# Padding of K and Q by DMA instead of Pool memsets, and a first LayerNorm in four batches, in a fused attention and GeGLU block

## Chip, cores and metric

One core of a Trainium2 chip. The metric is the device time of one execution in microseconds (us). Every kernel was run several times beside the kernel before on the same chip. Ratios are computed as the mean time of one kernel's fast runs over the mean of the other's fast runs of the same rounds, so they are not quite the ratios of the medians that are quoted. The kernel before differed from one section of runs to the next by up to 0.3% (medians 945.7 to 948.9 us, both on the same chip). This goes with the mean granted clock of PE that each run lists: over all sections 14 of its runs at 1.000 took 945.6 to 946.9 us, 10 at 0.998 took 947.1 to 948.0 and 10 at 0.996 took 948.9 to 949.2. So the ratios, and the times of events within a trace, carry the argument, not small differences of medians from different sections; and a ratio that is off 1 by a few tenths of a per cent says something only where both kernels ran at the same clock.

## The reference, cut to what matters

```python
# x: [1, 2048, 640] bf16; H = 32 heads of Dh = 20; Df = 1728
def reference(x, wqkv, wo, w_gate, w_up, w_down):
    n = layernorm(x)                                  # "LN1" below
    q, k, v = split_heads(n @ wqkv)                   # 32 heads x 2048 x 20
    p = softmax(q @ k.T * 20 ** -0.5)
    h = x + merge_heads(p @ v) @ wo
    m = layernorm(h)
    return h + (gelu(m @ w_gate) * (m @ w_up)) @ w_down
```

## The kernel before

The program is written as a list of operations with priorities. A list scheduler orders them for each engine with estimated durations before the program is built. The order on each engine is then fixed, and every engine works strictly in that order (in e5 below, LN1's third tile was ready at 14.57 us, but its transposes ran at 18.87, behind V projections that waited for their weights until 17.03).

K and Q lie transposed in SBUF. Partitions are used in four blocks of 32, one head in each: row 32j holds a bound, rows 32j+1 to 32j+20 the head's 20 values, rows 32j+21 to 32j+31 are padding. The padding must be written before the first scores are computed (0 in Q and about 1 in K). Heads come in 8 groups (`NG`); group 0 is started first.

```python
kt_all = sb("kt_all", [128, NG, S])            # K: 8 groups x 4 KB a partition
qt_all = sb("qt_all", [128, 4, NG, 512])       # Q: 4 chunks x 8 groups x 1 KB a partition

def fills(g0, g1, c0, c1):                     # Pool memsets of whole tiles, padding included
    v = lambda ap: ap.bitcast(FP32)
    n = g1 - g0
    cst(I("memset", v(kt_all[:, g0:g1, :].rearrange("p g s -> p (g s)")), ones2), "ktm%d" % g0, 1024 * n)
    for c in range(c0, c1):
        cst(I("memset", v(qt_all[:, c, g0:g1, :].rearrange("p g s -> p (g s)")), 0.0), "qtm%d%d" % (c, g0), 256 * n)

fills(0, 1, 0, 1)                              # group 0 first
# ... small constants ...
fills(1, NG, 0, 1)                             # then the rest of K and of Q's chunk 0
for c in range(1, 4):                          # and Q's chunks 1 to 3
    cst(I("memset", qt_all[:, c, :, :].rearrange("p g s -> p (g s)").bitcast(FP32), 0.0), "qtm%d" % c, 256 * NG)
# ...
def load(dst, src, key, mb, after=(), writes=None):          # all loads on the SP queue
    return op("sp", I("dma_start", dst, src), 0.08, P_BG, writes=writes or [key], after=after,
              sem=key, lat=2.2 + mb / 0.25)                  # the scheduler's estimate of the landing
for i in range(4):
    load_x(i)                                                # 0.65 MB each
load(wqk, A_wqkv[:, 0:1280]..., "wqk", 1.6)
load(wv, A_wqkv[:, 1280:1920]..., "wv", 0.8)
load(wo[:], ..., "wo", 0.8)
# ... LN1: statistics, scale and shift ("apply"), transposes through PE
for t0, n, eng in ((0, 4, "act"), (4, 4, "act"), (8, 8, "dve")):
    for t in range(t0, t0 + n):
        ln_stats(x_sb[:, t, :], t, [f"x{t // 4}"], P_BG)     # on DVE
    ln_rsqrt(t0, n, P_EPI, True)                             # square root on ScalarE
    for t in range(t0, t0 + n):
        e_ops.append(ln_apply(eng, x_sb[:, t, :], xn_p[:, t % 4, :], ("xnp", t % 4), t, [f"x{t // 4}"], P_EPI))
        transposes(xn_p[:, t % 4, :], [("xnp", t % 4)], xnT[:, :, t * 128:(t + 1) * 128], ("xnT", t),
                   ALLB, P_EPI, "act")                       # 5 PE transposes, then one evacuation
# ... projections of K and Q for group 0, rows moved into place by DMA
dma(kt_all[32 * j + 1:32 * j + 21, 0, 512 * c:512 * c + 512], src[DH * j:DH * j + DH, :], ...)   # per j and c
dma(qt_all[32 * j + 1:32 * j + 21, 0, 0, :], q_un[DH * j:DH * j + DH, 0, :], ("q", 0, 0, j), [("qu", 0), "qtm00"], ...)
# ... the bound add, the last step before the first scores: row 32j of group 0
op("dve", lambda eng: eng.scalar_tensor_tensor(out=qt_all[:, 0, 0, :], in0=bank(bk), scalar=off0[:, 0:1], in1=dst, ...),
   ..., reads=[key, "off0"] + q_keys[0][0], ...)
```

After this prologue ScalarE computes 719 exponentials of up to 1536 columns, one after the other, and a feed-forward tail follows.

## Time and profile before

| | kernel before |
|---|---|
| time, median of 4 runs | 946.96 us (946.62 to 947.25) |
| span of the profiled run | 943.9 us |
| ScalarE busy | 881.4 us (93%) |
| first exponential | 41.46 us after the span's start |
| last K evacuation of LN1 on ScalarE | 35.47 us |
| V weights landed | about 17.3 us |

The page of the kernel before, parts 1 and 4: busy time of each engine, and the chain of work that ended last, by engine.

```profile
PE 852.4 (90%) x10332; PEld 367.6 (39%) x10388; DVE 829.6 (88%) x1804; ACT 881.4 (93%) x789; POOL 17.9 (2%) x26
...
ACT 70%; PE 17%; DVE 12%; issue 0%; DMA 0%; DVEq 0%
```

Three engines look busy, but the chain is ScalarE's: whatever delays its first exponential delays the end by the same amount, as long as it runs without gaps afterwards. The timeline of ScalarE before, end of the prologue (columns: start, duration, engine, line, operation, output and input, count; in brackets the idle time before it and what ended it):

```profile
35.47 0.60 ACT L619 ACTIVATE regw<-ps 128x512 bf16<-128x512 f32 x1 [0.41 <-PE ps L592]
36.09 1.28 ACT L339 ACT_TABLE_LOAD   x1
41.46 4.62 ACT L339 ACTIVATE pts<-ps 128x1536 bf16<-128x1536 f32 x4 [4.09 <-PE ps L829]
```

The first line is the last K evacuation of LN1, the third the first exponentials. The whole prologue is the time to 41.46 us. The timeline of DVE and Pool before, in LN1:

```profile
6.00 6.08 POOL L339 MEMSET kt_all<- 128x7168 f32 x1
...
9.37 2.73 DVE L339 CAST mv<-mv 128x8 bf16<-128x8 f32 x1
...
12.13 7.18 POOL L339 MEMSET qt_all<- 128x1792 f32 x4
12.14 1.61 DVE L339 TENSOR_SCALAR sd<-mv 128x4 bf16<-128x4 bf16 x1
```

A cast of 8 elements takes 2.73 us: it stands still until Pool's memset of K ends at 12.08 us, and the next one waits for the first memset of Q. These stalls are what the change wants to remove. The timeline of PE before:

```profile
15.72 1.53 PE L556 MATMUL ps<-ident,rege 128*128 128x128 bf16 x10 [15.72 <-ACT rege L339]
17.32 2.02 PE L592 MATMUL ps<-regw 128*128 128x320 bf16 x7
```

After the transposes of the first two tiles, PE's fixed order has V projections (320 columns), and those start when the V weights have landed, at 17.3 us. The windows view before (columns as its first line says; the last is what the DMA engines moved):

```profile
core 0: us, PE busy (x) PEld busy (x) DVE busy (x) ACT busy (x) POOL busy (x), PEclk, DMA share, GB/s
8.00:19.00 11.00, 3.11 (x17) 1.90 (x18) 10.68 (x30) 4.46 (x7) 10.77 (x5) 1.00 1.01 357
19.00:33.00 14.00, 13.04 (x117) 8.49 (x118) 12.39 (x47) 12.47 (x22) 0.31 (x1) 1.00 0.04 9
112.00:118.00 6.00, 5.28 (x65) 1.36 (x57) 6.00 (x16) 6.00 (x7) 0.00 (x0) 1.00 0.51 113
```

Until 19 us the loads of x and of the weights keep all 16 DMA engines busy at 357 GB/s. Then the DMA engines are free. The last line is a transfer to 20 neighbouring partitions.

### The profile page before, as it was taken

The page shows a single profiled execution, that of the slowest core. Times are in us where ns is not written, and L with a number is a line of the kernel's source. Part 1 is how long each engine was busy: PE and PEld are TensorE (multiplying, and loading weights), DVE is VectorE, ACT ScalarE, POOL GpSimd, SP SyncE. Part 2 cuts the span into 40 slices and gives each one's busy share as a digit, 9 for nine tenths or more (in the row PEclk, how much of TensorE's full clock was granted, in tenths as well). Part 3 has the DMA queues.
Part 4 walks back from the last instruction along what each step waited for, and adds up shares of the span by engine and source line. Part 5 has one row for each costly group of instructions (what it writes and reads, how often), then busy time and mean ns, then how long its engine had stood idle before and what let it go on. Part 6 is the DMA issues. An engine that isn't in the chain of part 4 may idle for free.

```text
span 943.9 us, 23617 instructions
## 1 busy us (share of the span) xinstructions
PE 852.4 (90%) x10332; PEld 367.6 (39%) x10388; DVE 829.6 (88%) x1804; ACT 881.4 (93%) x789; POOL 17.9 (2%) x26
## 2 busy tenths in 40 slices
PE   2999999998898999998898997999999899999998
PEld 1533232222232223232243333344434446566577
DVE  8849999999799997988799999798999989989953
ACT  3799999999999999999999999999999999999931
POOL 7000000000000000000000000000000000000000
PEclk9999999999999999999999999999999999999999
DMA  7121102325500000001000000001100000000000
GB/s 250 51 73 35 52 15 67 92 59 156 181 1 1 1 1 1 1 15 42 1 3 1 2 1 1 1 2 30 30 1 2 2 15 18 3 17 10 3 22 16
DMA packets 22047, 30.13 MB, mean 32 GB/s; under 512 B 1964, under 2 KB 19464, under 8 KB 21944
## 3 DMA queue, kind: packets, MB, share of 16 engines
q1 hardware_dynamic: 21944, 28.63, 9.8%
q8 instruction: 81, 1.33, 0.6%
q14 instruction: 22, 0.18, 0.1%
HBM read 20.12 MB, written 8.09 MB: 30 GB/s over the span
## 4 chain that ended last, share of the span: by engine, by line
ACT 70%; PE 17%; DVE 12%; issue 0%; DMA 0%; DVEq 0%
ACT pts L339 45%; ACT rege L339 24%; PE ps L592 4%; DVE rege L339 4%; PE ps L1006 4%; PE ps L829 3%; PE ps L339 2%; PE ps L1057 2%; DVE rege L789 2%; DVE qt_all L339 2%; ACT L339 1%; DVE regw L622 1%; DVE stats L339 1%; PE ps L556 1%; DMA rege<-in_A_x_dram 0%
## 5 line engine op out<-in xcount | busy, mean ns | idle before, releaser
L339 ACT ACTIVATE pts<-ps 128x1536 bf16<-128x1536 f32 x480 | 572.2, 1368 | 8.4 <-PE ps L829 5.1
L829 PE MATMUL ps<-qt_all,kt_all 32*128 32x256 bf16 (+2 forms) x3584 | 304.0, 289 | 47.4 <-ACT pts L339 29.2
L339 ACT ACTIVATE rege<-ps 128x1536 bf16<-128x1536 f32 x239 | 298.9, 1369 | 1.7 <-PE ps L339 1.6
L829 PEld LDWEIGHTS ps<-qt_all,kt_all 32*128 32x128 bf16 x3584 | 96.0, 92 | 274.6 <-ACT pts L339 161.4
L339 DVE TENSOR_TENSOR qt_all<-qt_all 128x1024 bf16<-128x1024 bf16 (+1 forms) x240 | 164.1, 684 | 3.2
L1006 PE MATMUL ps<-rege,regw 128*128 128x256 bf16 (+2 forms) x955 | 146.4, 287 | 12.8 <-ACT rege L339 4.8
L339 PE MATMUL ps<-pts,v_all 128*21 128x256 bf16 (+2 forms) x2098 | 138.8, 290 | 0.9 <-DVE rege L339 0.5
L789 DVE TENSOR_SCALAR rege<-ps 128x512 int16<-128x512 f32 x154 | 105.4, 684 | 30.1 <-PE ps L829 29.1
L339 DVE TENSOR_SCALAR qt_all<-qt_all 128x1024 bf16<-128x1024 int16 (+1 forms) x288 | 115.6, 418 | 2.0
L339 PE MATMUL ps<-rege,v_all 128*21 128x256 bf16 (+2 forms) x1294 | 113.3, 292 | 0.0
L1006 PEld LDWEIGHTS ps<-rege,regw 128*128 128x128 bf16 x980 | 72.8, 98 | 63.4 <-issue 21.2
L592 PE MATMUL ps<-regw 128*128 128x320 bf16 (+1 forms) x342 | 81.5, 348 | 3.5 <-ACT regw L562 0.8
L1057 PE MATMUL ps<-regw,rege 128*128 128x320 bf16 x448 | 78.0, 301 | 1.9 <-DVE rege L1046 0.8
L339 PE MATMUL ps<-kt_all,zer 128*32 128x512 bf16 x824 | 70.6, 384 | 0.1
L789 DVE TENSOR_SCALAR qt_all<-ps 128x512 int16<-128x512 f32 x96 | 65.6, 685 | 3.2 <-PE ps L829 2.2
L339 DVE TENSOR_SCALAR rege<-rege 128x1024 int16<-128x1024 int16 (+2 forms) x166 | 67.3, 422 | 1.0
L339 DVE TENSOR_TENSOR rege<-rege 128x1024 bf16<-128x1024 bf16 (+3 forms) x103 | 66.1, 644 | 1.0
L339 PEld LDWEIGHTS ps<-pts,v_all 128*21 128x21 bf16 x2098 | 50.2, 91 | 38.4 <-issue 30.3
L1057 PEld LDWEIGHTS ps<-regw,rege 128*128 128x128 bf16 x448 | 36.9, 98 | 32.6 <-issue 15.2
L339 PEld LDWEIGHTS ps<-rege,v_all 128*21 128x21 bf16 x1294 | 41.1, 91 | 19.8 <-issue 14.3
L592 PEld LDWEIGHTS ps<-regw 128*128 128x128 bf16 x360 | 29.0, 98 | 45.9 <-issue 21.2
L1046 DVE TENSOR_TENSOR rege<-rege,ps 128x512 bf16<-128x512 bf16 (+1 forms) x53 | 35.8, 677 | 10.5 <-PE ps L1006 9.7
(86 smaller groups left out, 611.4 us busy)
## 6 DMA issues: line engine op xcount, KB each, us to landing
rege<-in_A_x_dram SPq DMA_DIRECT2D x6, 640.0 KB, 5.1
q_rows<-regw SPq DMA_DIRECT2D x20, 128.0 KB, 1.7
out_dram<-rege SPq DMA_DIRECT2D x16, 160.0 KB, 2.1
regw<-in_B_w_gate_dram SPq DMA_DIRECT2D x1, 2160.0 KB, 10.4
regw<-in_B_w_up_dram SPq DMA_DIRECT2D x1, 2160.0 KB, 15.4
regw<-in_B_w_down_dram SPq DMA_DIRECT2D x1, 2080.0 KB, 20.6
kt_all<-k_rows SPq DMA_DIRECT2D x12, 160.0 KB
qt_all<-q_rows SPq DMA_DIRECT2D x12, 160.0 KB
```

The source lines that it names most:

```text
L339: return lambda eng: getattr(eng, method)(*args, **kwargs)
L556: op("pe", lambda eng, a=a: eng.transpose(bank16(bk, D)[:, 128 * a:128 * a + 128], src[:, a * 128:(a + 1) * 128], ident[:]), 0.055, prio, ...
L592: yield op("pe", lambda eng, l=l, r=r, k=k: eng.matmul(bank(bk, n), l, r, start=(k == 0), stop=(k == len(steps) - 1)), c_mm(n), prio, mode ...
L622: e = op("dve", lambda eng: eng.tensor_copy(dst, bank(bk)), c_dve(512), prio, reads=[key], writes=[dkey], rel=[bk], after=after)
L789: d_ops.append(op("dve", lambda eng: eng.tensor_scalar(v[:, 512 * h:512 * h + 512], bank(b), EXP_MUL, -32000.0, ALU.mult, ALU.max), c_dve( ...
L829: return lambda eng: eng.matmul(out()[:, kk * nq:(kk + 1) * nq], kt_all[32 * j:32 * j + 32, g, kt * 128:(kt + 1) * 128], qt_all[32 * j:32 ...
L1006: op("pe", lambda eng, a=a, f=f, fi=fi: eng.matmul(bank(bk)[:, fi * nq:(fi + 1) * nq], w[:, a, F0[f]:F0[f] + 128], hnT[:, a, 128 * tb:128 ...
L1046: hdone.append(op("dve", lambda eng, bu=bu, fv=fv, w=w: eng.tensor_tensor(fv, fv, bank(bu, w), ALU.mult), c_dve(w), p, reads=[ku, ("ha", k ...
L1057: op("pe", lambda eng, f=f, o=o, hf=hf, bk=bk: eng.matmul(bank(bk, 320), ha_f[:, o:o + 128], wd[:, f, hf * 320:(hf + 1) * 320], start=(f = ...
```

## The change

Its intent: free DVE from the memsets by letting DMA copy the padding of group 0 to the other groups, start LN1's applies earlier with smaller batches, and share LN1's work more evenly between ScalarE and DVE. The diff, cut to its core:

```diff
-P_QK, P_PV, P_EPI, P_BG = 0, 1, 2, 3
+P_QK, P_PV, P_PRO, P_EPI, P_BG = 0, 1, 1.5, 2, 3
 ...
-        fills(0, 1, 0, 1)
+        cst(I("memset", kt_all[:, 0, :].bitcast(FP32), ones2), "ktm0", 1024)
+        cst(I("memset", qt_all[:, 0, 0, :].bitcast(FP32), 0.0), "qtm0", 256)
 ...
-        fills(1, NG, 0, 1)
-        for c in range(1, 4):
-            cst(I("memset", qt_all[:, c, :, :].rearrange("p g s -> p (g s)").bitcast(FP32), 0.0), "qtm%d" % c, 256 * NG)
 ...   (after the loads of x and the weights, on the same queue)
+        pad_rows = [(0, 1)] + [(32 * j + DH + 1, min(32 * j + 33, 128)) for j in range(4)]
+        k_fill = [("kfill", i) for i in range(len(pad_rows))]
+        q_fill = [("qfill", j) for j in range(4)]
+        for key, (a, b) in zip(k_fill, pad_rows):
+            op("sp", I("dma_start", kt_all[a:b, 1:NG, :], kt_all[a:b, 0:1, :].to_broadcast([b - a, NG - 1, S])), 0.72, P_BG,
+               reads=["ktm0"], writes=[key], sem="kf", lat=6.0)
+        for j, key in enumerate(q_fill):
+            a, b = 32 * j + DH + 1, 32 * j + 32
+            op("sp", I("dma_start", qt_all[a:b].rearrange("p c g s -> p (c g) s")[:, 1:4 * NG, :],
+                       qt_all[a:b, 0, 0:1, :].to_broadcast([b - a, 4 * NG - 1, 512])), 0.72, P_BG,
+               reads=["qtm0"], writes=[key], sem="qf", lat=4.0)
 ...
-        for t0, n, eng in ((0, 4, "act"), (4, 4, "act"), (8, 8, "dve")):
-            for t in range(t0, t0 + n):
-                ln_stats(x_sb[:, t, :], t, [f"x{t // 4}"], P_BG)
-            ln_rsqrt(t0, n, P_EPI, True)
+        for t0 in (0, 4, 8, 12):
+            if t0 == 4:
+                act_stats(4, 4)          # sums of x and x*x by two ScalarE passes a tile
+            else:
+                for t in range(t0, t0 + 4):
+                    ln_stats(x_sb[:, t, :], t, [f"x{t // 4}"], P_BG)
+            ln_rsqrt(t0, 4, P_PRO, sqrt=True)
 ...                                     # applies all on DVE; tiles 13 and 15 evacuated by DVE
+                           ALLB, P_PRO, "dve" if t in (13, 15) else "act")
 ...   (bound add of group 0: its tile is the source of the Q fills)
-               reads=[key, "off0"] + q_keys[0][0], writes=[("qo", 0, 0)], rel=[bk])
+               reads=[key, "off0"] + q_fill + q_keys[0][0], writes=[("qo", 0, 0)], rel=[bk])
 ...
-            proj_v(kt, 0, (6, 7), P_BG, "dve")
+            proj_v(kt, 0, (6, 7), P_EPI if kt < 8 else P_BG, "dve")
```

Later K and Q rows wait for `k_fill` and `q_fill` where they waited for the memsets.

More of the change, by code (lines that the diff above doesn't have):

```diff
@@ L360, in bass_sequential_preLN__mha_block__glu_gated_geglu__prompt_kernel @@
         rs = sb("rs", [128, NT], FP32)
-        nm = sb("nm", [128, NT], FP32)
+        nm = sb("nm", [128, 2], FP32)
+        asum = sb("asum", [128, 2, 4], FP32)
         mu = sb("mu", [128, NT], FP32)
@@ L408, in bass_sequential_preLN__mha_block__glu_gated_geglu__prompt_kernel @@
         xn_p = carve(4 * D).rearrange("p (i d) -> p i d", i=4)
+        junk = rege[:, 16000:16000 + D]
         carve = carver(rege, E_WORDS)
@@ L453, in bass_sequential_preLN__mha_block__glu_gated_geglu__prompt_kernel @@
         ones2 = 1.0019378662109375
-        def fills(g0, g1, c0, c1):
-            v = lambda ap: ap.bitcast(FP32)
-            n = g1 - g0
-            cst(I("memset", v(kt_all[:, g0:g1, :].rearrange("p g s -> p (g s)")), ones2), "ktm%d" % g0, 1024 * n)
-            for c in range(c0, c1):
-                cst(I("memset", v(qt_all[:, c, g0:g1, :].rearrange("p g s -> p (g s)")), 0.0), "qtm%d%d" % (c, g0), 256 * n)
-        fills(0, 1, 0, 1)
+        cst(I("memset", kt_all[:, 0, :].bitcast(FP32), ones2), "ktm0", 1024)
+        cst(I("memset", qt_all[:, 0, 0, :].bitcast(FP32), 0.0), "qtm0", 256)
         cst(I("memset", sel[:], -1.0), "sel", 160)
@@ L508, in ln_stats, with ln_rsqrt @@
             return [a, b]
-        def ln_rsqrt(t0, n, prio, need_nm=False, table=False):
+        def ln_rsqrt(t0, n, prio, table=False, sqrt=False):
             y = rs[:, t0:t0 + n]
@@ L519, in ln_rsqrt @@
             d(I("tensor_copy", mu[:, t0:t0 + n], mv16[:, 0:n, 0]), ["mv16"], [("mu", t) for t in ts])
-            if need_nm:
+            if sqrt:
                 op("act", I("activation", sd16[:, 0:n], sd16[:, 0:n], ACT.Sqrt), 0.2, prio, reads=["sd16"], writes=["sd16"])
                 d(I("reciprocal", y, sd16[:, 0:n]), ["sd16"], rk)
-                d(I("scalar_tensor_tensor", out=nm[:, t0:t0 + n], in0=y, scalar=-1.0, in1=mu[:, t0:t0 + n],
-                    op0=ALU.mult, op1=ALU.mult), rk + [("mu", t) for t in ts], [("nm", t) for t in ts])
                 return
@@ L574, in bass_sequential_preLN__mha_block__glu_gated_geglu__prompt_kernel, with act_stats @@
         ALLB = (7, 6, 0, 1, 2, 3, 4, 5)
-        for t0, n, eng in ((0, 4, "act"), (4, 4, "act"), (8, 8, "dve")):
+        def act_stats(t0, n):
             for t in range(t0, t0 + n):
-                ln_stats(x_sb[:, t, :], t, [f"x{t // 4}"], P_BG)
-            ln_rsqrt(t0, n, P_EPI, True)
-            for t in range(t0, t0 + n):
-                e_ops.append(ln_apply(eng, x_sb[:, t, :], xn_p[:, t % 4, :], ("xnp", t % 4), t, [f"x{t // 4}"], P_EPI))
+                for f, k in ((ACT.Copy, 0), (ACT.Square, 1)):
+                    op("act", I("activation", junk, x_sb[:, t, :], f, accum_out=asum[:, k, t - t0:t - t0 + 1]), 0.72, P_BG,
+                       reads=[f"x{t // 4}"], writes=["junk", ("as", t)])
+            m = mv[:, t0:t0 + n, 0]
+            rk = [("as", t) for t in range(t0, t0 + n)]
+            d = lambda fn, r, w: op("dve", fn, 0.17, P_EPI, reads=r, writes=w)
+            d(I("tensor_scalar", m, asum[:, 0, 0:n], 1.0 / D, None, ALU.mult), rk, ["am"])
+            d(I("tensor_tensor", asum[:, 0, 0:n], m, m, ALU.mult), ["am"], rk)
+            d(I("scalar_tensor_tensor", out=mv[:, t0:t0 + n, 1], in0=asum[:, 1, 0:n], scalar=1.0 / D, in1=asum[:, 0, 0:n],
+                op0=ALU.mult, op1=ALU.subtract), rk + ["am"], [("mv", t) for t in range(t0, t0 + n)])
+        for t0 in (0, 4, 8, 12):
[5 more added lines that the diff above has]
+            ln_rsqrt(t0, 4, P_PRO, sqrt=True)
+            for t in range(t0, t0 + 4):
+                e_ops.append(ln_apply("dve", x_sb[:, t, :], xn_p[:, t % 4, :], ("xnp", t % 4), t, [f"x{t // 4}"], P_PRO))
                 transposes(xn_p[:, t % 4, :], [("xnp", t % 4)], xnT[:, :, t * 128:(t + 1) * 128], ("xnT", t),
-                           ALLB, P_EPI, "act")
+                           ALLB, P_PRO, "dve" if t in (13, 15) else "act")
                 e_ops.append(len(sc.ops) - 2)
@@ L635, in proj_k @@
                             f"kc{c}", 2.2, prio)
-                dma(kdr[128 * t:128 * t + 128, 512 * c:512 * c + 512], src, ("kdr", t, c), [("ku", t % 2, c)], f"kw{c}", 2.7,
+                dma(kdr[128 * t:128 * t + 128, 512 * c:512 * c + 512], src, ("kdr", t, c), [("ku", t % 2, c)], f"kw{t % 2}{c}", 2.7,
                     max(prio, P_BG) if t == 0 else prio, 0.4)
@@ L658, in proj_k @@
                         kdr.rearrange("(g j e) s -> j e g s", j=4, e=DH)[j, :, g0:g1, :], ("k", t, j),
-                        [("kdr", tt, c) for tt in (t - 1, t) for c in range(4)] + ["ktm1"], f"k{t}", 2.2 + 1.0 * (g1 - g0), prio, keep=False)
+                        [("kdr", tt, c) for tt in (t - 1, t) for c in range(4)] + k_fill, f"k{t}", 2.2 + 1.0 * (g1 - g0), prio, keep=False)
             op("dve", I("tensor_reduce", kd[:, t:t + 1], ka[:, 0:256], AX.X, ALU.max), 0.33, prio, reads=[("ka", 0)],
@@ L673, in proj_q @@
                     dma(qt_all[32 * j + 1:32 * j + 21, 0, 0, :], q_un[DH * j:DH * j + DH, 0, :], ("q", 0, 0, j),
-                        [("qu", 0), "qtm00"], "qc", 2.2, prio)
+                        [("qu", 0), "qtm0"], "qc", 2.2, prio)
             dma(qdr[c, 128 * t:128 * t + 128, :], q_un[:, t, :], ("qdr", c, t), [("qu", t)], f"qw{t}", 2.7,
@@ L689, in q_bound @@
                reads=[key], writes=["qoff"], rel=[bk])
-            mk = "qtm%d" % c if c else "qtm01"
             dma(odr[c], qoff[0:32, :], ("odr", c, g0), ["qoff"], "ow", 2.5, prio, 0.4)
@@ L695, in q_bound @@
                     qdr[c].rearrange("(g j e) s -> j e g s", j=4, e=DH)[j, :, g0:g1, :], ("q", c, g0, j),
-                    [("qdr", c, t) for t in ts] + [mk], f"q{c}{g0}", 2.5, prio, keep=False)
+                    [("qdr", c, t) for t in ts] + q_fill, f"q{c}{g0}", 2.5, prio, keep=False)
             dma(qt_all[0:128:32, c, g0:g1, :], odr[c].rearrange("(g j) s -> j g s", j=4)[:, g0:g1, :], ("qo", c, g0),
-                [("odr", c, g0), mk], f"q{c}{g0}", 2.5, prio, keep=False)
+                [("odr", c, g0)] + q_fill, f"q{c}{g0}", 2.5, prio, keep=False)
             for g in range(g0, g1):
@@ L1069, in bass_sequential_preLN__mha_block__glu_gated_geglu__prompt_kernel @@
         PRO = ALLB
-        proj_k(0, PRO, P_EPI, "act")
-        proj_q(0, 0, PRO, P_EPI, "act")
-        q_bound0(PRO, P_EPI)
+        proj_k(0, PRO, P_PRO, "act")
+        proj_q(0, 0, PRO, P_PRO, "act")
+        q_bound0(PRO, P_PRO)
         sc.warm = I("matmul", PS[:, 512 * 7:512 * 8], kt_all[:, 0, 0:128], kt_all[:, 0, 0:512], start=True, stop=True,
```

## The prediction

It put the nine fills at 37 us together, one after another, 18 for K's and 19 for Q's, and so at 19 to 56 us, where "Sum" begins. This was an estimate. Two outcomes that would have refuted the forecast: 943 to 946 us with faster fills, near 1000 us with fills twice as slow.

> **What bounds it now.** The page shows ScalarE busy 881 of 944 us; the chain of waits gives it 70%, nearly all softmax exponentials (about 719 of 1.37 us). The timeline has the first exponential at 41.46 us and ScalarE almost gapless until about 892; then a feed-forward tail of 50 us. The diff touches only the prologue, so the time moves with the start of the first exponential, nearly one for one.
>
> **Removed.** Pool's big memsets (6.1 us for K, four of 1.8 us for Q, from 6.0 to 19.3 us). In the timeline DVE's small casts and tensor_scalars stand still beside them: 2.6 us at 9.4, 1.5 at 12.2 and about 2 after 16.8, each ending with a memset.[...] About 6 us go. Eight ScalarE applies (0.87 us, 7 us in all) become DVE applies (0.37 us); ScalarE gets eight sums instead (estimated 0.87 us each, early, while it is idle) and one table load more (1.28 us), and loses two of 16 evacuations (0.61 us). For LN alone I estimate the first exponential 0 to 4 us earlier: PE still waits for the V weights until 17.3 us.
>
> **Added: nine fill DMAs on the SP queue**, which I believe decide it. They stand behind x and the weights, whose bytes keep all 16 engines busy until 19.0 us (windows view). Each writes 11 or 12 neighbouring partitions: 344 KB per K fill, 349 KB per Q fill.[...] the two-group K loads (20 partitions, 4 x 164 KB, from 112.7 to 117.6 us) moved 655 KB in 4.9 us[...].[...] The first exponential needs them: the Q bound waits for all Q fills (row group 0 is their source), and group 0's K and Q rows stand behind them in the same queue.
>
> **Sum.** Fills end 56, rows landed 57, bound add 0.74, scores 0.5: first exponential near 58 instead of 41.5, +16.5 us. The LN gain is hidden behind this. Afterwards the order is nearly the old one, shifted.
>
> Predicted 964 us; 952 to 970 in 8 of 10. Faster by over 2%: 0.01; within: 0.67; slower: 0.32.
>
> **What shows it.** Timeline: no Pool memset over 1 us, no DVE cast of 2.6 us, the last LN apply and K evacuation earlier; an extra table load. Windows: about 80 GB/s from 19 to 56 us. Chain of waits: a DMA into Q or K, then the bound add at about 57; a ScalarE gap of over 10 us before the first exponential. Tail unchanged at 50 us.
>
> **What would make it wrong.**[...] Fills overtaking the weights: end near 46.[...]

## The result and the profile after

| | before | after |
|---|---|---|
| time, median | 946.96 us (946.62 to 947.25, 4 runs) | 962.23 us (961.36 to 963.47, 4 runs) |
| ratio | | 1.0162 (95% interval 1.0145 to 1.018) |
| span of the profiled run | 943.9 us | 959.5 us |
| first exponential | 41.46 us | 56.64 us |
| last K evacuation of LN1 | 35.47 us | 37.73 us |
| last input of the bound add to arrive | matmul at about 40.1 us | Q rows by DMA at 54.97 us |

The span grew by 15.6 us and the first exponential moved by 15.2 us: nearly the whole loss lies in the prologue. The page after, parts 1 and 4:

```profile
PE 865.0 (90%) x10339; PEld 368.1 (38%) x10339; DVE 828.9 (86%) x1806; ACT 881.9 (92%) x797; POOL 4.8 (1%) x21
...
ACT 78%; PE 14%; DVE 4%; DMA 1%; SPq 1%; issue 0%; DVEq 0%
```

Busy times moved little (PE's by 12.6 us), except Pool's, which lost its memsets. A page of busy times does not show this loss. The timeline of ScalarE after:

```profile
12.17 1.28 ACT L339 ACT_TABLE_LOAD   x1
...
37.73 0.60 ACT L637 ACTIVATE regw<-ps 128x512 bf16<-128x512 f32 x1 [1.42 <-PE ps L610]
...
56.64 4.97 ACT L339 ACTIVATE pts<-ps 128x1536 bf16<-128x1536 f32 x4 [17.01 <-PE ps L846]
62.70 2.37 ACT L339 ACTIVATE rege<-ps 128x1536 bf16<-128x1536 f32 x2 [1.09 <-PE ps L846]
```

LN1's last K evacuation is 2.3 us later than before, not earlier, and then ScalarE waits 17.0 us (4.1 before). The first line is a table load that the kernel before did not have. The chain of waits after names what ended the wait, a DMA that brings Q rows, and then the bound add:

```profile
46.42 8.55 DMA qt_all<-regw
...
55.17 0.75 DVE qt_all L726
```

The windows view after (columns as before):

```profile
8.00:19.00 11.00, 4.14 (x28) 3.12 (x29) 6.27 (x26) 9.56 (x20) 0.00 (x0) 1.00 1.06 372
19.00:33.00 14.00, 13.71 (x102) 8.17 (x101) 12.63 (x47) 7.65 (x15) 0.00 (x0) 1.00 0.76 86
33.00:51.00 18.00, 8.83 (x60) 4.60 (x57) 8.04 (x21) 3.29 (x4) 0.00 (x0) 0.81 0.77 80
51.00:55.00 4.00, 0.00 (x0) 0.00 (x0) 0.00 (x0) 0.00 (x0) 0.00 (x0) 0.50 0.79 175
55.00:60.00 5.00, 3.80 (x17) 0.82 (x17) 4.07 (x9) 3.22 (x3) 0.00 (x0) 0.50 0.32 99
```

From 19 to 51 us (9 GB/s from 19 to 33 us before) a share of 0.76 to 0.77 of the 16 engines (about 12 of them) is "busy" moving 80 to 86 GB/s. A busy DMA engine is not a fast one. From 51 us the rows that stood behind the fills come through at 175 GB/s. PE has meanwhile been idle for 14 us and its granted clock is at 0.50 (the column before the DMA share): in the trace's clock record from 44.33 to 61.40 us, over 5 us after PE worked again at 55.98. The gap of 1.09 us at 62.70 probably comes from this: e11 below shows a gap of 1.0 us at 81.68, too, with the clock at 0.50 from 75 to 80 us, and e4 one of 1.2 us at 86.82, after score matmuls that took 0.54 us for three at 82.58 (0.32 in e3 at 44.43). The timeline of the SP queue after shows the queue itself blocked:

```profile
8.29 7.04 SPq L339 DMA_DIRECT2D kt_all<-kt_all  x5
15.38 15.52 SPq L339 DMA_DIRECT2D qt_all<-qt_all  x4
30.94 13.15 SPq L339 DMA_DIRECT2D kt_all<-regw  x4
44.14 3.00 SPq L339 DMA_DIRECT2D qt_all<-regw  x4
```

Issuing four Q fills took 15.5 us, and the next four row copies 13.2 us, where the four after those took 3.0 us (3.6 and 3.0 us for the same two groups of four before). DVE after: the stalls are gone.

```profile
9.71 0.15 DVE L339 CAST mv<-mv 128x8 bf16<-128x8 f32 x1
...
33.48 1.51 DVE L339 TENSOR_SCALAR rege<-rege,mu,rs 128x640 bf16<-128x640 bf16 x4
```

The cast takes 0.15 us instead of 2.73. Yet the last applies end at 35.0 us, where the last ones before ended at 31.0 us. The timeline of DVE before:

```profile
28.10 2.94 DVE L339 TENSOR_SCALAR rege<-rege,mu,rs 128x640 bf16<-128x640 bf16 x8
```

### The profile page after: what moved, and what is told of

It reads as the page before. It is cut to its first block, busy times and chain, and to the rows that moved or that the text cites. A ratio compares the mean times of both kernels' runs of the same rounds, so it can differ in the third digit from the quotient of the medians.

```text
span 959.5 us, 23591 instructions
## 1 busy us (share of the span) xinstructions
PE 865.0 (90%) x10339; PEld 368.1 (38%) x10339; DVE 828.9 (86%) x1806; ACT 881.9 (92%) x797; POOL 4.8 (1%) x21
## 4 chain that ended last, share of the span: by engine, by line
ACT 78%; PE 14%; DVE 4%; DMA 1%; SPq 1%; issue 0%; DVEq 0%
ACT pts L339 50%; ACT rege L339 27%; PE ps L1023 4%; PE ps L610 3%; PE ps L846 2%; PE ps L1074 2%; PE ps L339 2%; DVE qt_all L339 2%; SPq L339 1%; ACT L339 1%; DMA qt_all<-regw 1%; PE ps L558 1%; DMA rege<-in_A_x_dram 1%; DVE rege L339 0%; DVE qt_all L806 0%; PE ps L702 0%
## 5 line engine op out<-in xcount | busy, mean ns | idle before, releaser
L1023 PE MATMUL ps<-rege,regw 128*128 128x256 bf16 (+2 forms) x980 | 152.9, 290 | 9.4 <-ACT rege L339 4.1
L1023 PEld LDWEIGHTS ps<-rege,regw 128*128 128x128 bf16 x980 | 72.8, 97 | 63.4 <-issue 21.4
L610 PE MATMUL ps<-regw 128*128 128x512 bf16 (+1 forms) x360 | 87.8, 356 | 0.8 <-DVE rege L806 0.2
L339 PE MATMUL ps<-kt_all,zer 128*32 128x512 bf16 x772 | 67.4, 385 | 0.0
```

Of the source, the lines that this page charges most:

```text
L339: return lambda eng: getattr(eng, method)(*args, **kwargs)
L610: yield op("pe", lambda eng, l=l, r=r, k=k: eng.matmul(bank(bk, n), l, r, start=(k == 0), stop=(k == len(steps) - 1)), c_mm(n), prio, mode ...
L1023: op("pe", lambda eng, a=a, f=f, fi=fi: eng.matmul(bank(bk)[:, fi * nq:(fi + 1) * nq], w[:, a, F0[f]:F0[f] + 128], hnT[:, a, 128 * tb:128 ...
```

## The experiments

All kernels gave correct results. "First exp." is the start of the first exponential in the profiled run.

| label | LN1 | padding | first exp., us | median, us | kernel before beside it, us | ratio |
|---|---|---|---|---|---|---|
| before | old | Pool memsets | 41.46 | 946.96 | | 1 |
| after | new | 9 narrow DMAs | 56.64 | 962.23 | 946.96 | 1.0162 |
| e1_pool_fill | new | Pool memsets | 46.29 | 949.73 | 948.93 | 1.0022 |
| e2_before_dma_fill | old | 9 narrow DMAs | 57.46 | 964.56 | 948.93 | 1.0171 |
| e3_wide_fill | new | 2 wide DMAs | 42.62 | 946.24 | 948.93 | 0.9982 |
| e14_e3_again | the same as e3 | | 42.50 | 947.07 | 946.70 | 1.0011 |
| e4_pool_queue | new | narrow, Pool's queue | 80.69 | 985.88 | 948.93 | 1.0398 |
| e10_narrow_nowait | new | narrow, bound add need not wait | 54.54 | 960.32 | 945.66 | 1.0152 |
| e11_narrow_half | new | narrow, 24/31 of Q later | 42.89 | 957.99 | 948.87 | 1.0103 |
| e5_before_staged | old | wide, in two stages | 42.24 | 947.29 | 945.66 | 1.0012 |
| e8_before_staged_land | old, true landing times | wide, in two stages | 38.32 | 943.97 | 945.66 | 0.9978 |
| e13_e8_again | the same as e8 | | 39.78 | 944.31 | 946.70 | 0.9975 |
| e9_after_land_tab | new, repaired | wide, in two stages | 41.35 | 944.94 | 945.66 | 0.9990 |
| e12_before_vlate | as e8, V still later | wide, in two stages | 39.16 | 948.18 | 948.87 | 0.9997 |

The means of the runs at clock 1.000 alone are: kernel before 945.9 us (14 runs), e1 949.6 (3), e3 and e14 together 946.0 (6), e5 946.5 (1), e8 and e13 together 943.7 (7), e9 944.9 (2), e12 948.1 (5). The kernels with narrow fills have no run at 1.000.

Two theories stood at the start. Mine: the narrow fills hold up the first exponential, and LN1 does not matter. The rival: the reordered LN1 itself costs the time.

### Which half of the change costs it: e1 and e2

e1 puts the memsets back into the changed kernel:

```diff
-        (the nine fill DMAs)
+        cst(I("memset", kt_all[:, 1:NG, :]..., ones2), "kfillp", 1024 * (NG - 1))
+        (and four memsets of Q, as before)
```

> The changed kernel with the padding written by Pool memsets again; LN1 as changed. Theory (the narrow fills hold up the first exponential): the gap before it closes; in the changed kernel PE had the bound matmul done at 41.7 us, so the first exponential is at 43 to 46 us (DVE stalls beside the memsets come back) and the time is 948 to 952 us. Rival (the new LN1 order costs the time itself): still about 962 us.

Measured: 949.73 us, ratio 1.0022. The timeline of ScalarE in e1:

```profile
46.29 4.62 ACT L339 ACTIVATE pts<-ps 128x1536 bf16<-128x1536 f32 x4 [3.46 <-PE ps L840]
```

The ScalarE wait is back to 3.5 us, so the wait of 17 us belongs to the fills. The new LN1 beside Pool's memsets is 4.8 us later than the old one beside them, probably because all its applies are on DVE as well. The ratio shows only 2 us of this, since no run of the kernel before was at clock 1.000 in that section; at clock 1.000 e1 is 3.7 us slower. So e1 alone doesn't clear the new LN1; e2 and e3 do.

e2 does the opposite, the nine narrow DMAs and their waits in the kernel before.

> The kernel before with only the padding changed to the nine narrow DMA fills. Theory: fills end near 51 us, group 0's rows land at 54 to 55, first exponential near 56 us, 960 to 963 us. Rival (LN1 costs it): DVE's stalls of some 6 us go and nothing else changes, so 941 to 945 us.

Measured: 964.56 us, ratio 1.0171, a little above the stated range, in a section where the kernel before was also 2 us slower. (PE's half clock also lasted longer, to 66.4 us in its trace, whose mean granted clock is 0.989 against 0.991 after, with gaps of 2.5 us in all after the first exponentials.) The timeline of ScalarE in e2:

```profile
57.46 3.84 ACT L339 ACTIVATE pts<-ps 128x1536 bf16<-128x1536 f32 x3 [18.93 <-PE ps L837]
```

The fills alone cost as much as the whole change. The rival theory falls.

### Bytes, engines or partitions: e3

In e3 the changed kernel writes the padding over all 128 partitions with one DMA for K and one for Q (7.1 MB instead of 2.8 MB; rows that hold data are overwritten later). The source is group 1, which Pool memsets as well. Queue and waits stay the same.

```diff
-        (nine DMAs over 1, 11 or 12 partitions)
+        op("sp", I("dma_start", kt_all[:, 2:NG, :], kt_all[:, 1:2, :].to_broadcast([128, NG - 2, S])), ...)
+        op("sp", I("dma_start", qt_all.rearrange("p c g s -> p (c g) s")[:, 2:4 * NG, :],
+                   qt_all[:, 0, 1:2, :].to_broadcast([128, 4 * NG - 2, 512])), ...)
```

> The changed kernel with each fill made over all 128 partitions (source: group 1, memset by Pool too), 7.1 MB instead of 2.8 MB, same queue, same waits. Theory[...]:[...] done near 35 us, no longer than LN1 needs; first exponential near 43 us, about 948 us although 2.5 times the bytes move. Rival (each DMA engine limited to the 7 GB/s seen in the narrow fills, or descriptors or bytes count): 63 us or more, 985 us or slower.

Measured: 946.24 us, ratio 0.9982; five more rounds (e14) gave 1.0011. The 0.9982 was a matter of the clock: three of e3's four runs were at 1.000 and none of the kernel before beside it.

> The same kernel as e3 (the changed kernel with wide fills) again, five rounds. Its first exponential is 1.2 us later than before and its gaps afterwards are no smaller, so the 0.998 of the first time should be chance: 0.999 to 1.003. If 0.998 holds, something after the first exponential improved that the gaps don't show.

The timeline of ScalarE and the windows view of e3:

```profile
42.62 4.62 ACT L339 ACTIVATE pts<-ps 128x1536 bf16<-128x1536 f32 x4 [3.54 <-PE ps L843]
```

```profile
19.00:27.00 8.00, 7.71 (x62) 4.62 (x61) 7.23 (x29) 4.22 (x9) 0.00 (x0) 1.00 1.03 403
27.00:37.00 10.00, 10.00 (x82) 6.00 (x80) 9.48 (x30) 4.84 (x9) 0.00 (x0) 1.00 1.09 349
```

Two and a half times the bytes took 18 us instead of 32, at 349 to 403 GB/s instead of 80 to 86. It is not the bytes, the queue, or a limit of each engine. What is left is how many partitions a fill touches: 11 or 12 against 128. The 4096-byte packets, each of which goes to one partition, have the durations that go with the rates. In the changed kernel's K fills their median is 611 ns, which is 6.7 GB/s; in the wide fills it is 164 ns (25 GB/s, and the windows view's 403 GB/s over 16 engines comes to the same), so it is no limit of one partition either. Of the 336 packets of the K fills 207 took 575 to 675 ns, but 19 took 150 to 200 ns; why these were quick was not shown. A weaker sign is the transfer in the kernel before, four loads to 20 neighbouring partitions each: 113 GB/s over its window of 6 us, idle edges included, though it is not shown that the four ran one after another. By which mechanism a narrow fill is slow was not shown. The DMA share of 0.76 to 0.77 of 16 would be about 12 engines, but does not tell 12 from 11, for this share reads 1.01 to 1.09 when all 16 are busy.

### The wait or the queue: e10

In e10 the narrow fills copy from group 1, so that the bound add, which overwrites group 0, need not wait for them.

```diff
-               reads=[key, "off0"] + q_fill + q_keys[0][0], ...
+               reads=[key, "off0"] + q_keys[0][0], ...
```

> The changed kernel with the narrow fills copying from group 1 (a second memset by Pool) so that the bound add need not wait for the Q fills; everything else as changed, the fills 1/7 to 1/31 smaller. Theory (group 0's K and Q rows stand behind the fills in the same queue): fills end near 49 us, rows land near 52, first exponential 52 to 56 us, 957 to 963 us. Rival (the added wait for the Q fills is the cost): first exponential near 43 us, 947 to 949 us.

Measured: 960.32 us, ratio 1.0152. The timeline of ScalarE in e10:

```profile
54.54 4.94 ACT L339 ACTIVATE pts<-ps 128x1536 bf16<-128x1536 f32 x4 [14.84 <-PE ps L848]
```

The explicit wait is worth nothing: the rows of group 0 stand behind the fills in the queue anyway. The 2 us that it gained are about what the shorter fills account for.

### Another queue: e4

e4 issues the same narrow fills from Pool's queue, in front of no row and beside the loads.

```diff
-            op("sp", I("dma_start", kt_all[a:b, 1:NG, :], ...
+            op(POOL, I("dma_start", kt_all[a:b, 1:NG, :], ...
```

> The changed kernel with the nine narrow fills issued from Pool's queue. Theory:[...] the fills end at 42 to 48 us and group 0's rows no longer stand behind them; first exponential 44 to 50 us, 949 to 957 us; weights land up to 3 us later. Rival (only the sum of bytes behind the loads matters, or the wait is SP's blocked queue): if SP's block alone counted, first exponential near 43 us, 948 us; if the start doesn't matter, 962 us.

Measured: 985.88 us, ratio 1.0398. This was a bad miss: none of the stated outcomes. The windows view of e4, and its chain of waits:

```profile
8.00:16.00 8.00, 0.00 (x0) 0.00 (x0) 0.74 (x3) 5.34 (x11) 2.34 (x9) 1.00 1.09 124
30.00:50.00 20.00, 0.00 (x0) 0.00 (x0) 0.00 (x0) 0.00 (x0) 0.00 (x0) 1.00 1.07 114
```

```profile
21.50 32.80 another core or an unknown queue
...
54.43 6.03 PE ps L610 x23
```

The PEclk column reads 1.00 here although PE stands idle: the trace of e4 records its first change of clock only at 58.4 us, and before the first record the column shows 1.00. All 16 engines are "busy" (share 1.07 to 1.09) at 114 to 124 GB/s, where the loads alone moved 357 between 8 and 19 us before. PE's first V projection, which waits for the V weights, starts at 54.4 us instead of 17.3. The loads were slowed to the pace of the narrow fills. The runs show only the effect, not the mechanism: e4 changed the queue and the start of the fills at once. In the changed kernel the fills at least stood behind the loads, and its time was 23.7 us less (962.23, in another section).

### How much fill is too much: e11

e11 issues the narrow Q fills of chunks 1 to 3 only after the bound add (from a small zero tile), leaving 58% of the fill time in front (15.2 + 4 of 33 us).

> The changed kernel, narrow fills as changed, but the Q fills of chunks 1 to 3 (24 of the 31 rows a partition) are issued only after the bound add. In the changed kernel the K fills took 15.2 us and the Q fills 17.5; now 15.2 + 17.5 x 7/31 = 19.2 us, done near 38 us. Theory: group 0's rows land near 40, LN1 is then the limit (42.6 us in the kernel with wide fills): first exponential 42.5 to 44.5 us, 946 to 950 us, some 13 us less than the changed kernel. Rival (a fixed cost of filling by this queue[...]): stays above 955 us.

Measured: 957.99 us, ratio 1.0103. The timeline of ScalarE in e11:

```profile
42.89 4.62 ACT L339 ACTIVATE pts<-ps 128x1536 bf16<-128x1536 f32 x4 [3.51 <-PE ps L849]
...
78.16 2.52 ACT L339 ACTIVATE pts<-ps 128x1536 bf16<-128x1536 f32 x2 [7.82 <-PE ps L849]
81.68 2.36 ACT L339 ACTIVATE pts<-ps 128x1536 bf16<-128x1536 f32 x2 [0.99 <-PE ps L849]
```

The first exponential came where it was expected: the fills in front ended near 38 us (86 GB/s from 34 to 38 us, 154 from 38 to 42), no longer than LN1 needs. The total missed: the deferred fills now stand in front of group 1's rows, and ScalarE waits 8.8 us at 78 us. The time of the narrow fills was moved, and most of the gain was given back later.

### What the removal of the stalls is worth: e5 and e8

e5 keeps the old LN1 and takes the memsets away without narrow fills: K and Q's chunk 0 by wide DMAs, Q's chunks 1 to 3 by one more after the bound add.

> The kernel before, LN1 untouched, padding by wide DMA fills over 128 partitions (K and the first Q chunk at once, 3.9 MB done near 29 us; the other Q chunks after the first exponential). Removes the Pool memsets without the narrow fills. Theory A (PE waits until 17.2 us for the V weights whatever DVE does, so the stalls beside the memsets were hidden): first exponential 41 to 43 us, 945 to 949 us. Theory B (the stalls of 6 us counted, as their place in the chain of waits suggests): first exponential 35 to 38 us, 940 to 943 us.

Measured: 947.29 us, ratio 1.0012, first exponential 42.24 us: theory A. The timeline of PE in e5:

```profile
12.31 1.52 PE L562 MATMUL ps<-ident,rege 128*128 128x128 bf16 x10 [12.31 <-ACT rege L339]
17.03 2.05 PE L598 MATMUL ps<-regw 128*128 128x320 bf16 x7 [3.20 <-DMA regw<-in_A_wqkv_dram]
```

The first transposes come 3.4 us earlier than in the kernel before (12.31 instead of 15.72), as they should without the stalls. But the V projection next in PE's order still starts at 17.03 us, because the V weights land then. The stalls beside the memsets lay in front of a wait that was there anyway. They stood in the chain of waits of the kernel before, for they happened to end it last, but only a little of them was worth anything. (PE's slow start, explained at e13 below, took about 1 us more in e5's trace than in that of the kernel before: its next eight V matmuls took 2.21 us instead of 1.25. Without this the first exponential would be about level with the one before, still no gain.)

The cause is the scheduler's estimate: it takes each load to land at 2.2 us plus its own bytes over 250 GB/s after its issue, as if the loads did not share the DMA engines, so about 6 us for the V weights; they land at 17.3. e8 is e5 with the landing times of the trace:

```diff
-                      sem=key, lat=2.2 + mb / 0.25)
+                      sem=key, lat=LAND.get(key, 2.2 + mb / 0.25))
+        LAND.update(x0=4.3, x1=6.2, x2=8.0, x3=9.5, wqk=13.8, wv=16.2, wo=17.8)
```

> As e5, and the scheduler is told when x and the weights really land (x 5 to 10 us, Q/K weights 14.7, V weights 17.3) instead of 5 to 9 us, so it puts no V projection ahead of the transposes of LN1. If the PE's wait for the V weights is what hides the gain: first exponential 36 to 40 us, 941 to 945 us. If PE or the evacuations on ScalarE bound LN1 anyway: 41 to 43 us, 946 to 949 us.

Measured: 943.97 us, ratio 0.9978, first exponential 38.32 us, 3.1 us earlier than before. The timelines of ScalarE and of PE in e8:

```profile
38.32 4.62 ACT L339 ACTIVATE pts<-ps 128x1536 bf16<-128x1536 f32 x4 [4.09 <-PE ps L838]
```

```profile
16.00 0.71 PE L566 MATMUL ps<-ident,rege 128*128 128x128 bf16 x5 [0.69 <-ACT rege L339]
17.00 3.25 PE L602 MATMUL ps<-regw 128*128 128x320 bf16 x10 [0.29 <-DMA regw<-in_A_wqkv_dram]
...
20.36 0.81 PE L602 MATMUL ps<-regw 128*128 128x512 bf16 x3
```

PE now transposes all four tiles of the first batch before it waits for the V weights, and waits 0.29 us for them instead of 3.20. Five more rounds on another chip:

> The same kernel as e8 again, five rounds, to see whether its 0.2% holds on another chip: first exponential 38.3 us, 0.997 to 0.999 of the kernel before. If it was chance: 1.000 or more.

Measured: 944.31 us, ratio 0.9975 (95% interval 0.9962 to 0.9988); first exponential 39.78 us, 1.5 us later than expected. It is a gain of a quarter of a per cent, and the best version: it beats both kernels. At clock 1.000 alone it is 2.2 us (943.7 against 945.9), so the clock does not explain it. The timeline of PE in e13 shows where the 1.5 us went:

```profile
17.07 3.96 PE L602 MATMUL ps<-regw 128*128 128x320 bf16 x10 [0.29 <-DMA regw<-in_A_wqkv_dram]
...
21.36 1.28 PE L602 MATMUL ps<-regw 128*128 128x512 bf16 x3
```

The same three matmuls took 0.81 us in e8, at full clock, and 1.28 us in e13, still at half. The traces record PE's first change to full clock at 19.4 us in e8 and 22.3 us in e13 (19.2 us in the kernel before, 21.4 in e5, 21.2 in e9, 23.1 in e12). So the first exponential of one profiled run can lie 1 to 2 us off for this reason alone, and the 3.1 us of e8 against the kernel before is a fair comparison, for PE reached full clock at about the same time in both.

### What the new LN1 is worth: e9, and a step too far: e12

e9 gives the new LN1 the wide fills (its bound add need not wait for them) and the landing times of e8, and loads the square-root table at the very start, so that the table load at 12.17 us goes away.

> The changed kernel's LN1 with the wide staged fills of e5, the real landing times of e8, and the square-root table loaded first (no second load in the middle). If these three faults hid what the new LN1 gives: first exponential 36 to 40 us, 940 to 945 us, and faster than e8. If the new LN1 has no worth: as e8 or slower.

Measured: 944.94 us, ratio 0.9990, first exponential 41.35 us. With its faults repaired the new LN1 is 1.6 to 3.0 us later to the first exponential than the old one in e13 and e8, and about 1 us slower in time at clock 1.000. Sharing the work out anew brought nothing here. The extra table load of the changed kernel, gone here, took 1.28 us.

e12 is e8 with V told to land later still, so that no V projection stands in front of the K projections.

> As e8 (LN1 of before, wide staged fills, real landing times), with the V weights told to land 2.3 us later still, so that no V projection stands before the K projections of the prologue on PE. If PE's in-order queue is what bounds LN1: first exponential 34 to 37.5 us, 939 to 943 us, faster than e8. If ScalarE's evacuations bound it: as e8, 38 us, 943 to 945 us; the V projections moved behind the first exponential may give some of it back as gaps.

Measured: 948.18 us, ratio 0.9997, first exponential 39.16 us. It missed: the first exponential is no earlier, and the V projections moved behind it give gaps there. The first part is not a fair test, for PE came to full clock 3.7 us later than in e8 (eight matmuls of 512 columns from 17.55 us took 3.60 us; eight in the kernel before, at full clock, 1.90). The time is clear: at clock 1.000 e12 is 2.2 us slower than the kernel before, though the ratio, with the kernel before mostly at 0.996 to 0.998, hides it. The timeline of ScalarE in e12:

```profile
46.61 4.62 ACT L339 ACTIVATE pts<-ps 128x1536 bf16<-128x1536 f32 x4 [0.56 <-PE ps L339]
```

Four more gaps of 1.1, 2.3, 1.2 and 2.0 us before 181 us all end with a matmul of the probabilities with V.

## Why the prediction was right, and where it was not

- **The time.** 964 us predicted, 962.23 measured, inside the range of 952 to 970, with 0.67 given to "within 2%". The main step, that nine narrow fills decide the change, is shown by e1, e2 and e3 together. That the total came within 2 us is partly luck, as the next two points show.
- **The size of the fills.** Predicted 37 us, done at about 56. In the trace the 4096-byte packets of the K fills run from 18.2 to 34.5 us (16.3 us; 18 predicted), and the rate stays near 80 GB/s until about 51 us, so about 33 us in all: I predicted 4 us too much, mostly in the Q fills. I added the fills up as if none overlapped. The rate rises above 90 GB/s at 26 to 28 us (94 and 123) and at 43 to 45 us (114 and 98), about where the second of four fills gives over to the third; so some overlap there is possible, but not shown packet by packet.
- **The rows behind the fills.** 1 us allowed; the Q rows landed at 54.97, about 4 us after the fills' end. This term was too small by 3 us, and the two errors nearly cancelled: first exponential predicted near 58, measured 56.64.
- **The slowness of the fills.** That it goes with the few partitions that a fill touches is shown by e3 (more bytes, less time) and by the packet durations (611 ns against 164). The reason that the prediction gave was not shown. That the Q bound waits for the fills was named as a cause beside the queue; e10 shows that the queue alone does it.
- **"For LN alone I estimate the first exponential 0 to 4 us earlier."** This failed. Without the narrow fills (e3) the first exponential is at 42.6 us, 1.2 later than before, and in the changed kernel the last K evacuation is at 37.73 instead of 35.47, where I had written that it would be earlier. The prediction saw that PE waits for the V weights until 17.3 us, but still credited the stalls; e5 shows that their removal alone gives nothing (42.24), and e8 that it gives 3.1 us once the order is mended.
- **DVE's stalls, the extra table load, the unchanged tail.** As predicted: the cast fell from 2.73 to 0.15 us; a load of 1.28 us appeared at 12.17; the loss is all in front of the first exponential but for 0.4 us. Not foreseen was the half clock after PE's idle time, with its gap of about 1 us.

What stays open: by which mechanism the narrow fills are slow and slowed the loads in e4, whether e12's order would bring the first exponential forward with PE at full clock as early as in e8, and why PE comes to full clock at a different time in each run.

## What to carry to other kernels

Cost a DMA within SBUF by the partitions it touches, not by its bytes alone: here a copy to 11 neighbouring rows ran at 80 GB/s, one to all 128 at about 390, so writing 2.5 times the bytes was nearly twice as fast, and the row copies queued behind the narrow copies (after) and the loads running beside them (e4) waited for them. A stall that stands in the chain of waits is worth its length only if nothing behind it was waiting for something else; look at what the next engine's fixed order needs next, here the V weights. When a scheduler fixes the order, check its estimates of DMA landings against the trace first: correcting seven numbers (e8 against e5) gave more than redesigning the LayerNorm. And before a difference of a few us is explained, compare the granted clock of the two runs.
